# Input order, instruction order and the banks of the last output halves in a recurrence and feed-forward kernel on one core

## The chip, the core and the metric

The kernel runs on one core of a Trainium2 chip. A core has a matrix engine (PE, TensorE), a vector engine (DVE), a scalar engine (ACT), a general engine (POOL, GpSimd) and a queue engine (SP) that only issues transfers; each runs its own list of instructions in order, and semaphores hold an instruction until what it needs is done. Transfers between main memory and the on-chip SBUF are issued by SP and by POOL and carried by 16 DMA engines that all queues share. PE writes its results to PSUM, eight banks of 128 x 512 float32, from which DVE and ACT read. The metric is the device time of one execution in microseconds (us), lower is better.

## What is computed

A gated recurrence for 4 batches, 8 heads, 768 steps and head width 48, whose output goes, token by token, through a feed-forward layer of 384 to 2048 to 384 with SiLU:

```python
f = 1.0 / (1.0 + np.exp(-f_logit))
for t in range(S):
    state = f[:, :, t, :, None] * state + np.einsum('bhd,bhe->bhde', k[:, :, t], v[:, :, t])
    y[:, :, t] = np.einsum('bhd,bhde->bhe', q[:, :, t], state)
x = y.transpose(0, 2, 1, 3).reshape(B * S, H * D)
h = x @ w_in
out = (h * (1.0 / (1.0 + np.exp(-h)))) @ w_out
```

## The kernel before

The 768 steps of each batch are cut into six chunks of 128, so that there are 24 units (batch, chunk). Two units make a pair, and the 12 pairs are numbered 0 to 11. Pairs 0 to 3 hold two chunks of the same batch ("T" pairs, whose tokens are laid alternately over two slots); pairs 4 to 11 hold the same chunk of two batches. Within a chunk the recurrence is done with matmuls: the logarithm of the gate is summed along the chunk by a triangular matmul, q and k are scaled by the exponentials of that sum, scores of q against k are masked and applied to v, and a 48 x 48 state per head carries what came before.

The whole order of the kernel is written out by hand, in a table of words (`PLAN`, from line 37). A word is `kind.pair.part:engine:buffer`; the letters P, A, V, G and S stand for PE, ACT, DVE, POOL and SP. Each engine runs its own words in the order of the table. The kinds that matter here, with the line that issues them before the change:

- `f`, `k`, `q`, `v` (L241): a load of 384 KB from SP's queue, or half of one; `wi.n` and `wo.n` (L216, L219): a quarter of the first or second weight matrix, from POOL's queue, with a cast to bfloat16. Only the first four loads of the table are issued ahead of the setup of masks and constants.
- `E` (L248) and `L` (L260, L263): the exponential and the logarithm on ACT that make the log gate out of f. `cs` (L324 and L328 in T pairs, L331 and L334 in the others): its running sum on PE.
- `a`, `ia` (L336): the exponentials of that sum, on ACT; `al` (L278, L338): the decay over the whole chunk.
- `qg`, `ki` (L341): q times `a` and k times `ia`, on DVE or POOL. `vb`: v cast to bfloat16, on any of ACT, DVE and POOL.
- `tq` (L348): transposes of scaled q and k on PE; `qkc`: their copy out of PSUM on ACT or DVE (`qkD` has the DMA transpose them instead, L360).
- `sc` (L369, L373): scores; `at` (L377): their masking on DVE, in two halves per unit.
- `d` (L297, L406): a chunk's contribution to the state; `sd`, `su` (L410, L420): the state's update. `y`, `yi` (L285, L385, L389): the outputs of a chunk. `yc`, `yT`, `xc` (L397): cast, transpose and copy into the input of the feed-forward layer.
- `mi.P.j` (L271): the first weight matrix, 256 of the 2048 columns at a time; with a third number, for one unit of the pair only. `si` (L276): SiLU on ACT. `mo.P.i.n` (L306): a quarter of the second weight matrix. `oc`: the copy of the result out of PSUM; `so` (L316, L318): the store, from SP's or POOL's queue.
- `idle.512.n` (L465): n matmuls of zeros, 512 columns wide, whose result nobody reads.

For the last pair, `mo`, `oc` and `so` carry a further number: each of its two output tiles is made in two column halves of 192, and both halves of a tile lie in one bank of PSUM:

```python
nc.tensor.matmul(at("o", P, i)[:, cols], at("hT", P)[:, n, i * C:(i + 1) * C], w_out_sb[:, n, cols], start=(n == 0), stop=(n == NT - 1))
```

Of the kernel before, what the change touches and what calls it, by code (L numbers as in the profile page):

```python
# [41 lines left out]
tq.1.0:P:2 q.3.0:S:3 a.2.0:A:3 qg.1.1:G: sc.0.0:P:3,4 qkc.1.0:A:1 sc.0.1:P:6,7 at.0.0.1:V:0 k.3.0:S:3 wi.1:G: at.0.0.0:V: E.3.0:A:1 idle.512.2::5
tq.1.1:P:5 at.0.1.0:V:1 wi.2:G: d.1:P:1,4 qkc.1.1:A: v.2.0:S:2 su.1.0:V:0 wi.0:G: at.0.1.1:V: al.2:A:2 L.3.0:A:0 idle.512.3::2 sc.1.0:P:2,3 ki.2.0:G:4
sc.1.1:P:6,1 at.1.0.1:V:2 vb.0.0:A:2 cs.3.1:P:5 vb.0.1:A:3 at.1.1.0:V:3 qg.2.0:G: al.3:A:3 ia.2.1:A:2 d.0:P:7,3 at.1.1.1:V: a.2.1:A:0 cs.3.0:P:6
ia.3.1:A:4 su.0.0:V:0 qg.2.1:G:2 y.0:P:0,1 a.3.0:A:1 at.1.0.0:V: yc.0.0:A:0 yi.0.1:P: tq.2.0:P:7 a.3.1:A:3 wi.3:G: yc.0.1:V:1 ia.3.0:A:0 y.1:P:0,2
# [64 lines left out]
def kernel(  # L110
# [19 lines left out]
    NT = d_ff // 128  # L130
# [35 lines left out]
    for word in PLAN.split():  # L166
        name, eng, got = word.split(":")
# [257 lines left out]
    def takes(kind, rest):  # L425
# [22 lines left out]
        if kind == "mo":  # L448
            return [("o", *rest[:2])]
# [97 lines left out]
```

## Time and profile before

| what | before |
|---|---|
| median of 3 runs | 181.83 us |
| lowest and highest run | 181.17 and 182.06 us |
| the profiled execution's own time | 180.93 us |
| its span, first to last instruction | 179.2 us |
| PE busy in the span | 170.5 us (95%) |
| ACT, DVE, POOL busy | 132.7, 79.7, 61.6 us |
| granted TensorE clock | 1.000 |
| bytes moved | 31.91 MB |

PE is the busiest engine. A row of the profile that groups instructions gives the line, the engine, the operation, what is written and read, the count, the busy time and the mean time of one, and then the idle time of the engine just before these instructions. In rows by time, the first number is the start in us from the start of the span and the second the time until the group's end; consecutive instructions of one kind are merged. Instructions of one engine can overlap by about 0.1 us, so the distance from start to start is what one of them costs its engine.

### The profile page before, as it was taken

Reading aid. Unit: us, or ns where it says so; the run is one execution under the profiler, and the core shown is the slowest. Engines: PE = TensorE matmul, PEld = TensorE weight load, DVE = VectorE, ACT = ScalarE, POOL = GpSimd, SP = SyncE. Lnnn points to the kernel's source line nnn. Section 1 sums busy time; section 2 is a strip of 40 time slices with the busy share of each in tenths; the row PEclk is TensorE's granted clock in tenths of the full one; section 3 lists DMA queues with packets and bytes.
Section 4 is the critical chain, followed back from the end, with each engine's and each line's share of the span. In section 5 each row is a group of like instructions: output and inputs, shape, how many; then the busy total and the mean of one; then the engine's idle time right before and its main releaser. Section 6 shows DMA issues by size and latency. Waiting matters only on the chain.

```text
span 179.2 us, 4981 instructions
## 1 busy us (share of the span) xinstructions
PE 170.5 (95%) x2042; PEld 129.0 (72%) x2044; DVE 79.7 (44%) x166; ACT 132.7 (74%) x251; POOL 61.6 (34%) x106
## 2 busy tenths in 40 slices
PE   6769989999999999999999999999999999999993
PEld 2345779975788866778678877875876786788782
DVE  7078994008821246456673703342335747500002
ACT  3989983895289999999967558988796991178410
POOL 6036995000274004554044170636303592000010
PEclk9999999999999999999999999999999999999999
DMA  6999999999999799998478998994994496320043
GB/s 159 324 325 325 240 204 207 199 187 190 242 230 212 92 208 221 168 241 144 84 145 170 188 210 141 252 263 103 179 251 94 97 190 215 88 70 0 0 150 117
DMA packets 109366, 31.91 MB, mean 178 GB/s; under 512 B 103536, under 2 KB 108768, under 8 KB 109344
## 3 DMA queue, kind: packets, MB, share of 16 engines
q1 hardware_dynamic: 104464, 25.60, 70.2%
q0 software_dynamic: 4880, 6.00, 15.7%
q8 instruction: 16, 0.26, 0.6%
q14 instruction: 6, 0.05, 0.1%
HBM read 25.17 MB, written 4.72 MB: 167 GB/s over the span
## 4 chain that ended last, share of the span: by engine, by line
PE 77%; ACT 9%; DVE 4%; DMA 3%; SPq 2%; issue 1%; POOL 1%; DVEq 0%
PE pb L306 32%; PE pb L271 32%; ACT hT L276 4%; DMA q<-in_q_dram 3%; PE pb L373 2%; SPq L241 2%; PE pb L385 2%; PE pb L348 2%; PE pb L389 2%; DVE qk L341 2%; ACT L513 1%; DVE atm L377 1%; PE pb L331 1%; PE pb L397 1%; DVE st L420 1%
## 5 line engine op out<-in xcount | busy, mean ns | idle before, releaser
L306 PE MATMUL pb<-w_out_sb,hT 128*128 128x384 bf16 (+1 forms) x416 | 70.4, 314 | 0.2 <-ACT hT L276 0.2
L271 PE MATMUL pb<-xT,w_in_sb 128*128 128x256 bf16 (+1 forms) x672 | 68.9, 257 | 0.0
L271 PEld LDWEIGHTS <-w_in_sb 128*128 128x128 bf16 x672 | 56.6, 98 | 7.5 <-issue 0.3
L276 ACT ACTIVATE hT<-pb 128x512 bf16<-128x512 f32 x96 | 51.8, 617 | 12.4 <-PE pb L271 12.0
L306 PEld LDWEIGHTS <-hT 128*128 128x128 bf16 x416 | 37.7, 98 | 18.7 <-ACT hT L276 0.4
L377 DVE TENSOR_TENSOR atm<-pb,triu 128x512 bf16<-128x512 f32 x32 | 20.6, 684 | 20.5 <-PE pb L373 17.8
L336 ACT ACTIVATE x<-pb 128x384 f32<-128x384 f32 x48 | 22.1, 508 | 1.5 <-PE pb L331 1.4
L420 POOL TENSOR_TENSOR st<-sd,al 48x192 bf16<-48x192 f32 x32 | 16.6, 518 | 18.7 <-PE pb L385 12.1
L341 POOL TENSOR_TENSOR qk<-q,x 128x384 bf16<-128x384 f32 x11 | 11.3, 1025 | 31.9 <-ACT x L336 14.5
L513 ACT ACT_TABLE_LOAD x15 | 19.2, 1283 | 0.3
L185 ACT COPY ob<-pb 128x384 f32<-128x384 f32 (+1 forms) x15 | 6.8, 453 | 12.6 <-PE pb L306 12.6
L377 DVE TENSOR_TENSOR atm<-pb,mask 128x512 bf16<-128x512 f32 x16 | 10.2, 685 | 12.4 <-ACT hT L276 11.1
L187 DVE COPY ob<-pb 128x384 f32<-128x384 f32 (+1 forms) x11 | 5.8, 535 | 22.2 <-PE pb L306 22.2
L318 POOL DMA_DIRECT2D out_dram<-ob x8 | 4.6, 578 | 28.4 <-ACT ob L185 24.8
L316 POOL DMA_DIRECT2D out_dram<-ob x14 | 7.6, 548 | 19.6 <-DVE ob L187 15.9
L341 DVE TENSOR_TENSOR qk<-q,x 128x384 bf16<-128x384 f32 x13 | 7.6, 593 | 13.7 <-ACT x L336 13.7
L248 ACT ACTIVATE e<-f 128x768 f32<-128x768 f32 (+1 forms) x13 | 10.4, 800 | 4.4 <-DMA f<-in_f_logit_dram 4.2
L410 DVE TENSOR_TENSOR sd<-pb,st 128x384 f32<-128x384 f32 x16 | 8.9, 554 | 10.6 <-PE pb L406 3.9
L341 POOL TENSOR_TENSOR qk<-k,x 128x384 bf16<-128x384 f32 x10 | 10.8, 1082 | 6.4 <-ACT al L278 2.0
L185 ACT CAST yb<-pb 128x384 bf16<-128x384 f32 x12 | 5.6, 479 | 9.7 <-PE pb L389 9.6
L341 DVE TENSOR_TENSOR qk<-k,x 128x384 bf16<-128x384 f32 x14 | 9.9, 710 | 0.9 <-ACT x L336 0.9
L187 DVE CAST yb<-pb 128x384 bf16<-128x384 f32 x12 | 6.6, 556 | 8.0 <-PE pb L389 5.9
(72 smaller groups left out, 157.4 us busy)
## 6 DMA issues: line engine op xcount, KB each, us to landing
f<-in_f_logit_dram SPq DMA_DIRECT2D x11, 384.0 KB, 4.7
q<-in_q_dram SPq DMA_DIRECT2D x16, 192.0 KB, 4.1
v<-in_v_dram SPq DMA_DIRECT2D x16, 192.0 KB, 3.9
k<-in_k_dram SPq DMA_DIRECT2D x16, 192.0 KB, 3.9
k<-in_k_dram SPq DMA_DIRECT2D x4, 384.0 KB, 4.8
v<-in_v_dram SPq DMA_DIRECT2D x4, 384.0 KB, 9.5
q<-in_q_dram SPq DMA_DIRECT2D x4, 384.0 KB, 4.9
w_in_sb<-in_moe_w_in_dram POOLq DMA_DIRECT2D x4, 384.0 KB, 9.5
```

The costliest lines, as they stand in the source:

```text
L185: nc.scalar.copy(dst, src)
L187: ENG[eng].tensor_copy(dst, src)
L248: return nc.scalar.activation(e, at("f", P)[:, j * w:(j + 1) * w], AF.Exp, scale=-1.0)
L271: nc.tensor.matmul(h[:, i, cols], w_in_sb[:, kk, n * 128:(n + 1) * 128], at("xT", P)[:, kk, cols], start=(kk == 0), stop=(kk == KT - 1))
L276: return nc.scalar.activation(at("hT", P)[:, 2 * j:2 * j + 2, :], at("h", P, j).rearrange("p (n c) -> p n c", n=2), AF.Silu)
L306: nc.tensor.matmul(at("o", P, i)[:, cols], at("hT", P)[:, n, i * C:(i + 1) * C], w_out_sb[:, n, cols], start=(n == 0), stop=(n == NT - 1))
L336: nc.scalar.activation(at(kind, P, i).rearrange("p h d -> p (h d)"), at("cs", P, i)[:, 0:HD], AF.Exp, scale=1.0 if kind == "ia" else -1.0)
L341: ENG[eng].tensor_mul(at("qk", P, i)[:, j, :, 0:D], heads("qk"[j], P, i), at("ia" if j else "a", P, i))
L377: ENG[eng].tensor_mul(at("atm", P, i)[:, r], at(f"s{r}", P, i).rearrange("p (n c) -> p n c", c=C), mask[:, None, :].to_broadcast([C, NP, C]))
L410: nc.vector.tensor_add(at("sd", P, i), d_ps, prev_state(P, i))
L420: ENG[eng].tensor_mul(at("st", P, i)[lo:lo + D, :, r * D:(r + 1) * D], src[lo:lo + D, :, r * D:(r + 1) * D], al_of(P, i)[lo:lo + D, :, Non ...
L513: nc.scalar.preload_act_table_set(TABLES[mode])
```

## The change

The table is replaced by another one, and three lines of code give each half of the last pair's outputs a bank of its own. The counts of work stay as they are, but for these: 29 instead of 24 matmuls of zeros; of the copies out of PSUM, three `qkc` and four `xc` go from ACT to DVE and four `yc` from DVE to ACT; ten `vb` instead of five lie on POOL; two `ki` go from DVE to POOL; two stores go from POOL's queue to SP's; ACT has 13 loads of its function table behind the first one, where it had 15.

```diff
-f.2.0:S:0 k.0.0:S:0 f.0.1:S:1 f.0.0:S: E.2.0:A:0 f.1.0:S:2 L.2.0:A:0 v.1.0:S:0 q.0.0:S:0 idle.512.11::0 cs.2.1:P:0 E.0.1:A:1 E.0.0:A: k.1.0:S:1
...
-wo.0:G: ki.2.1:V: yc.1.0:A:2 yT.0.0:P:5 sd.0.1:V:0 yi.1.1:P: yT.0.1:P:1 yc.1.1:A:0 tq.2.1:P:6 xc.0.0:V:0 wo.1:G: xc.0.1:A: qkc.2.0:V:0 v.3.0:S:3
-yT.1.0:P:0 yT.1.1:P:3 xc.1.0:A:1 mi.0.2.0:P:2 qkc.2.1:V: su.0.1:G:0 xc.1.1:A: mi.0.3.0:P:5 mi.1.3.0:P:1 sd.1.1:V:1 mi.1.3.1:P: qg.3.0:V:3 wo.2:G:
...
+k.0.0:S:0 f.2.0:S:0 f.0.1:S:1 f.0.0:S: f.1.0:S:2 v.1.0:S:0 q.0.0:S:0 E.2.0:A:0 E.0.1:A:1 k.1.0:S:1 L.0.1:A:0 E.0.0:A: L.0.0:A: f.3.0:S:3
...
+yc.1.0:V:2 tq.2.0:P:4 yT.0.1:P:6 yi.1.1:P: wo.3:G: xc.0.1:V: yT.1.0:P:3 yc.1.1:A:0 sd.0.1:V:0 mi.0.2.1:P:6 al.3:A:3 ia.3.1:A:4 xc.1.0:V:1 mi.0.5.0:P:5
+wo.2:G: a.3.0:A:2 sd.1.1:V:1 mi.0.3.0:P:2 mi.1.4.0:P:3 qkc.2.0:V:0 qg.3.1:G:3 mi.0.5.1:P: v.5.1:S:4 mi.0.2.0:P: yT.1.1:P:7 su.0.1:G:0 mi.0.3.1:P:
+si.0.2:A:0 xc.1.1:V: mi.1.5.1:P:1 tq.2.1:P:0 su.1.1:G:0 mi.1.3.0:P:4 qkc.2.1:V: mi.1.3.1:P: mi.0.4.1:P:7 ki.3.0:G:0 mi.0.4.0:P: mi.1.5.0:P: si.0.4:A:
...
-                nc.tensor.matmul(at("o", P, i)[:, cols], at("hT", P)[:, n, i * C:(i + 1) * C], w_out_sb[:, n, cols], start=(n == 0), stop=(n == NT - 1))
+                nc.tensor.matmul(at("o", P, i, *rest[3:])[:, cols], at("hT", P)[:, n, i * C:(i + 1) * C], w_out_sb[:, n, cols], start=(n == 0), stop=(n == NT - 1))
...
-            copy(eng, at("ob", P, i)[:, cols], at("o", P, i)[:, cols])
+            copy(eng, at("ob", P, i)[:, cols], at("o", P, i, *rest[2:])[:, cols])
...
-            return [("o", *rest[:2])]
+            return [("o", *rest[:2], *rest[3:])]
```

In the new table the last `tq` of pair 2 (`tq.2.1`) and the last `yT` of pair 1 (`yT.1.1`) stand behind the first `mi` on PE, where they stood ahead of it.

The first place is SP's queue of loads, at its start. Buffers are named by kind and number: f_61, f_62, f_63 and f_64 take f of pairs 2, 0, 1 and 3, k_65 and q_71 are those of pair 0, k_66, q_72 and v_77 those of pair 1, v_78 that of pair 0. Before:

```order
L241 DMA f_61<-in_f_logit_dram 128x8x96
L241 DMA k_65<-in_k_dram 128x8x96
L241 DMA f_62<-in_f_logit_dram 128x4x96 x2
L241 DMA f_63<-in_f_logit_dram 128x8x96
L241 DMA v_77<-in_v_dram 128x8x96
L241 DMA q_71<-in_q_dram 128x8x96
L241 DMA k_66<-in_k_dram 128x8x96
L241 DMA q_72<-in_q_dram 128x8x96
L241 DMA f_64<-in_f_logit_dram 128x8x96
L241 DMA v_78<-in_v_dram 128x8x96
```

And with the change:

```order
L240 DMA k_65<-in_k_dram 128x8x96
L240 DMA f_61<-in_f_logit_dram 128x8x96
L240 DMA f_62<-in_f_logit_dram 128x4x96 x2
L240 DMA f_63<-in_f_logit_dram 128x8x96
L240 DMA v_77<-in_v_dram 128x8x96
L240 DMA q_71<-in_q_dram 128x8x96
L240 DMA k_66<-in_k_dram 128x8x96
L240 DMA f_64<-in_f_logit_dram 128x8x96
L240 DMA q_72<-in_q_dram 128x8x96
L240 DMA k_67<-in_k_dram 128x8x96
```

k of pair 0 and f of pair 2 change places at the head; f of pair 3 goes ahead of q of pair 1, and v of pair 0 goes from tenth place among whole loads to twelfth, behind k and q of pair 2.

The second place is ACT's list from its first exponential on. e_83 and lf_85 are the intermediate and the log gate of the pair loaded first; x is `a` or `ia`. Before:

```order
L248 ACTIVATE e_83<-f_61 128x768
L260 ACTIVATE lf_85<-e_83 128x8x2x48
L248 ACTIVATE e_84<-f_62 128x384 x2
L260 ACTIVATE lf_86<-e_84 128x4x2x48 x2
L248 ACTIVATE e_83<-f_63 128x768
L336 ACTIVATE x_88<-pb_142 128x384
L260 ACTIVATE lf_87<-e_83 128x8x2x48
L336 ACTIVATE x_89<-pb_143 128x384
L336 ACTIVATE x_90<-pb_143 128x384
L336 ACTIVATE x_91<-pb_144 128x384
L278 ACTIVATE al_128<-pb_145 128x8
L336 ACTIVATE x_92<-pb_142 128x384
```

And with the change:

```order
L247 ACTIVATE e_83<-f_61 128x768
L247 ACTIVATE e_84<-f_62 128x384
L259 ACTIVATE lf_85<-e_84 128x4x2x48
L247 ACTIVATE e_84<-f_62 128x384
L259 ACTIVATE lf_85<-e_84 128x4x2x48
L247 ACTIVATE e_84<-f_63 128x768
L259 ACTIVATE lf_86<-e_84 128x8x2x48
L335 ACTIVATE x_88<-pb_140 128x384
L335 ACTIVATE x_89<-pb_141 128x384
L335 ACTIVATE x_90<-pb_140 128x384
L335 ACTIVATE x_91<-pb_143 128x384
L259 ACTIVATE lf_87<-e_83 128x8x2x48
```

The exponential of pair 2's f still comes first; its logarithm (lf_87 now) goes from second place to twelfth, and the logarithm of pair 1 now comes ahead of the first `a`.

The third place is DVE's list from the masking of pair 0 to the last masking of pair 1; atm_111 and atm_112 belong to pair 0, atm_113 and atm_114 to pair 1, and st is the state. Before:

```order
L377 TENSOR_TENSOR atm_111<-pb_144,mask_159 128x512
L377 TENSOR_TENSOR atm_111<-pb_143,mask_159 128x512
L377 TENSOR_TENSOR atm_112<-pb_146,mask_160 128x512
L420 TENSOR_TENSOR st_149<-pb_141,al_128 48x4x48 x2
L377 TENSOR_TENSOR atm_112<-pb_147,mask_160 128x512
L377 TENSOR_TENSOR atm_113<-pb_143,mask_159 128x512
L377 TENSOR_TENSOR atm_114<-pb_146,mask_160 128x512
L377 TENSOR_TENSOR atm_114<-pb_141,mask_160 128x512
L420 TENSOR_TENSOR st_148<-pb_147,al_129 48x4x48 x2
L377 TENSOR_TENSOR atm_113<-pb_142,mask_159 128x512
```

And with the change:

```order
L419 TENSOR_TENSOR st_149<-pb_147,al_128 48x4x48 x2
L376 TENSOR_TENSOR atm_111<-pb_143,mask_160 128x512
L376 TENSOR_TENSOR atm_111<-pb_142,mask_160 128x512
L376 TENSOR_TENSOR atm_112<-pb_145,mask_159 128x512
L186 CAST vb_101<-v_78 128x384
L186 COPY qkTT_110<-pb_147 128x16x64
L376 TENSOR_TENSOR atm_112<-pb_146,mask_159 128x512
L419 TENSOR_TENSOR st_148<-pb_143,al_129 48x4x48 x2
L376 TENSOR_TENSOR atm_113<-pb_145,mask_160 128x512
L376 TENSOR_TENSOR atm_113<-pb_141,mask_160 128x512
L376 TENSOR_TENSOR atm_114<-pb_143,mask_159 128x512
L376 TENSOR_TENSOR atm_114<-pb_145,mask_159 128x512
```

The state of pair 1 (st_149) is updated first instead of after three maskings, and a cast of v and a copy of transposed q and k, which lay on ACT, stand between the maskings.

More of the change, by code (lines that the diff above doesn't have):

```diff
@@ L42 @@
[L42 to L45, printed above, removed]
@@ L106 @@
+mo.11.1.2.0:P: so.11.0.0:G: mo.11.1.2.1:P: mo.11.1.3.0:P: mo.10.0.3:P: oc.11.1.0:A:0 so.11.1.0:S: mo.11.0.0.1:P:7 oc.10.0:V:2 so.9.0:S: mo.11.1.3.1:P:
+so.10.0:S: mo.11.0.1.1:P: oc.11.1.1:V: mo.11.0.2.1:P: so.11.1.1:S: mo.11.0.3.1:P: oc.11.0.1:A: so.11.0.1:S:
 """
```

122 lines of the change are left out of this document (61 added, 61 removed).

## The prediction

> **What bounds the kernel now.** I read the page's first part, then the busy time by stretch, then the chain of waits, then the engines one by one through the first 25 us.
>
> ```profile
> PE 170.5 (95%) x2042; PEld 129.0 (72%) x2044; DVE 79.7 (44%) x166; ACT 132.7 (74%) x251; POOL 61.6 (34%) x106
> ```
>
> The busy time by stretch has, after the stretch and its length, the engines in this order: PE, weight loads, DVE, ACT, POOL.
>
> ```profile
> 10.00:15.00 5.00, 4.38 (x70) 2.65 (x72) 4.31 (x7) 4.51 (x13) 1.17 (x2) 1.00 1.17 325
> 15.00:20.00 5.00, 4.36 (x107) 2.93 (x97) 4.73 (x9) 5.00 (x11) 4.98 (x6) 1.00 1.18 306
> 20.00:25.00 5.00, 4.93 (x128) 4.50 (x127) 4.96 (x12) 4.85 (x12) 4.87 (x8) 1.00 1.21 205
> 40.00:60.00 20.00, 19.88 (x281) 15.28 (x272) 10.76 (x24) 13.86 (x27) 6.62 (x11) 1.00 1.03 212
> 60.00:80.00 20.00, 19.78 (x201) 13.61 (x198) 8.76 (x16) 19.88 (x39) 6.52 (x11) 1.00 1.11 188
> 170.00:175.00 5.00, 5.00 (x52) 4.22 (x50) 0.67 (x2) 0.64 (x2) 0.55 (x1) 1.00 0.45 157
> ```
>
> From 40 us on PE has hardly a gap: 0.12 + 0.22 us in the two stretches to 80 and nothing at the end; the stretches between show none either. Its work does not change, so there an order can give back about 0.34 us and no more, but a worse order can lose. The other place is the head, before the first matmul of the feed-forward layer, where PE runs zeros and waits. There DVE is the full engine (4.73 of 5, 4.96 of 5). The chain shows how it is fed:
>
> ```profile
> 5.24 4.81 DMA q<-in_q_dram
> 17.87 2.48 DVE atm L377 x4
> 21.82 0.52 PE pb L285 x32
> 22.79 0.17 PE pb L397 x3
> 22.95 0.45 PE pb L348 x8
> ```
>
> q of pair 0 lands at 10.05, DVE multiplies and masks, and PE can take the outputs of pair 1 (L285) once the last masking is done. On PE itself:
>
> ```profile
> 23.58 1.84 PE L271 MATMUL pb<-xT,w_in_sb 128*128 128x128 bf16 x30
> 26.72 0.36 PE L369 MATMUL pb<-qkTT 48*64 48x128 bf16 x11 [0.85 <-issue]
> ```
>
> The feed-forward layer starts at 23.58 and is stopped once more, for 0.85 us, inside one group of scores; "issue" says that the profile shows nothing that PE waited for.
>
> **The change part by part.** Most of it is the order of the head, so I rebuild that chain from starts in the trace. First ACT, which makes the factors DVE needs:
>
> ```profile
> 4.05 0.84 ACT L248 ACTIVATE e<-f 128x768 f32<-128x768 f32 x1 [2.03 <-DMA f<-in_f_logit_dram]
> 4.92 0.84 ACT L260 ACTIVATE lf<-e 128x768 bf16<-128x768 f32 x1
> 5.83 1.18 ACT L248 ACTIVATE e<-f 128x384 f32<-128x384 f32 x2
> 6.91 0.92 ACT L260 ACTIVATE lf<-e 128x384 bf16<-128x384 f32 x2
> 7.73 0.83 ACT L248 ACTIVATE e<-f 128x768 f32<-128x768 f32 x1
> 8.47 0.47 ACT L336 ACTIVATE x<-pb 128x384 f32<-128x384 f32 x1
> 8.84 0.83 ACT L260 ACTIVATE lf<-e 128x768 bf16<-128x768 f32 x1
> 9.57 1.24 ACT L336 ACTIVATE x<-pb 128x384 f32<-128x384 f32 x3
> 12.02 0.91 ACT L336 ACTIVATE x<-pb 128x384 f32<-128x384 f32 x2
> ```
>
> *The two first loads swapped.* A load is 393 KB and the queue moves 325 GB/s (first row of the stretches), 1.21 us each. ACT's first exponential waited for f of pair 2 until 4.05; as second load that f lands at 5.26, and ACT's list still begins with it, so all behind it starts late. From 5.26: a full exponential costs ACT 0.74 until the next independent operation (7.73 to 8.47); a logarithm that needs the exponential just ahead comes 0.55 (half width) or 0.87 (4.05 to 4.92) after it; other half-width ones follow at about 0.42; a logarithm costs 0.73 (8.84 to 9.57); an `a` or `ia` 0.37 (8.47 to 8.84). Then: halves of pair 0 at 6.00, 6.55, 6.98, 7.53; pair 1 at 7.95 and 8.82; the first `a` at 9.55 (8.47 before). Three more `a` and `ia` to 10.66, the moved logarithm of pair 2 at 11.03, three `ia` from 11.76, half a us (estimated from the `ia` steps, since both are no longer than one) for `al` and a cast of v, and `a` of pair 1 at 13.35, ending at 13.84. Before, it was the second of the pair at 12.02 and ended at 12.93. So the factor of pair 1 comes 0.9 us later.
>
> *DVE from there.*
>
> ```profile
> 10.62 0.55 DVE L341 TENSOR_TENSOR qk<-k,x 128x384 bf16<-128x384 f32 x1
> 11.09 0.55 DVE L341 TENSOR_TENSOR qk<-q,x 128x384 bf16<-128x384 f32 x1
> 11.56 1.36 DVE L341 TENSOR_TENSOR qk<-k,x 128x384 bf16<-128x384 f32 x1
> 12.84 0.68 DVE L187 COPY qkTT<-pb 128x1024 bf16<-128x1024 bf16 x1
> 13.44 0.54 DVE L341 TENSOR_TENSOR qk<-q,x 128x384 bf16<-128x384 f32 x1
> 17.12 0.72 DVE L420 TENSOR_TENSOR st<-pb,al 48x192 bf16<-48x192 f32 x2 [0.17 <-PE pb L297]
> 17.87 2.48 DVE L377 TENSOR_TENSOR atm<-pb,mask 128x512 bf16<-128x512 f32 x4
> 20.27 0.71 DVE L420 TENSOR_TENSOR st<-pb,al 48x192 bf16<-48x192 f32 x2
> 21.02 0.69 DVE L377 TENSOR_TENSOR atm<-pb,mask 128x512 bf16<-128x512 f32 x1
> 21.63 0.55 DVE L187 CAST yb<-pb 128x384 bf16<-128x384 f32 x1
> ```
>
> q times `a` of pair 1 starts at 13.87, k times `ia` 0.47 later (10.62 to 11.09), ending at 14.89. `d` of pair 1 follows on PE, and the state's update, which is now ahead of the maskings on DVE, starts 0.62 after it:
>
> ```profile
> 16.50 0.52 PE L297 MATMUL pb<-vb,qk 64*128 64x96 bf16 x16
> ```
>
> (16.50 to 17.12), that is at 15.53. From here DVE has no hole that I can find: two updates at 0.75 (17.12 to 17.87), eight maskings at 0.60 (17.87 to 20.27, four), and the two pieces that came over from ACT, a cast at 0.46 (priced as the cast at 21.63, to the next start at 22.09) and a copy of 1024 columns at 0.60 (12.84 to 13.44). Sum 1.50 + 4.80 + 0.46 + 0.60 = 7.36, so the last masking ends at 22.98 instead of 21.71: 1.27 later. Behind it come `y` of pair 1 (0.63 until its end, 21.71 to 22.34 in the chain's L285 row), the cast (0.55), a transpose and the first `mi` (0.25 with hand-overs): 24.45, say **24.5 instead of 23.58, +0.92**. It makes up 0.35 of the 1.27 because `mi` no longer waits for the transposes that were moved behind it.
>
> *Work moved behind the start.* `tq.2.1` and `yT.1.1` now come after the first `mi`: 0.45 and 0.17 (chain rows at 22.95 and 22.79). PE is full from there, so **+0.62**.
>
> *The stop of 0.85.* The scores of pair 2 where it fell now come some 9 us later, among matmuls of 128 columns. It can vanish (-0.85) or come back elsewhere (0). I take **-0.5**, nearer to vanishing, since dense groups of small matmuls no longer follow one another there.
>
> *ACT's relief.* Two table loads (1.28 each, by the chain) and some copies leave ACT, which is full from 60 to 80. PE loses only 0.22 us in that stretch. Between 0 and -0.34 over all; I take **-0.1**.
>
> *The rest at nothing.* The five more matmuls of zeros lie in waits: five at 0.40
>
> ```profile
> 1.37 4.37 PE L465 MATMUL pb<-zero,triu 128*128 128x512 bf16 x11 [1.37 <-POOL triu masks.py:66]
> ```
>
> (4.37 for 11) end by 7.8, and the first `cs` cannot start before the second half logarithm ends, at 8.05; without that cover, up to 2 us. The halves in banks of their own end no wait, since PE is 5.00 of 5.00 busy in the last stretch and the store after the last matmul is the same.
>
> Sum: 0.92 + 0.62 - 0.5 - 0.1 = +0.94, about **+1.0 us**. The profiled execution took 180.93 (span 179.2), 0.9 below the median of 181.83; I carry the difference to the median: **182.8**.
>
> *A rule beside it.* The row at 11.56 took 1.36 where its neighbours take 0.55, and POOL's multiplication ran from 11.44 to 12.50:
>
> ```profile
> 11.44 1.06 POOL L341 TENSOR_TENSOR qk<-k,x 128x384 bf16<-128x384 f32 x1 [2.04 <-ACT al L278]
> 15.83 2.46 POOL L216 DMA_DIRECT2D w_in_sb<-in_moe_w_in_dram  x3
> ```
>
> The Trainium skill, page "SBUF — State Buffer", section "Who interferes with whom", says that a DVE instruction with two SBUF inputs and a GpSimd instruction that reads SBUF exclude each other for a whole instruction; the row agrees. By that rule the larger share of POOL speaks against the change: if POOL's cast of v follows its multiplication without letting DVE in, k times `ia` of pair 0 slips, and the sum would be 0.4 us higher. Without it the sum stands as above.
>
> **The rivals.** *The weights collide with the inputs* (slower, and more). POOL's three requests for the first weight go out right after k times `ia` and a cast, and no longer behind a second multiplication: `ia` of pair 1 ends at 12.3, the multiplication takes 1.06, the cast about half of that, so at 13.9 instead of 15.83. When weights flow, SP's loads crawl:
>
> ```profile
> k<-in_k_dram SPq DMA_DIRECT2D x4, 384.0 KB, 4.8
> v<-in_v_dram SPq DMA_DIRECT2D x4, 384.0 KB, 9.5
> DMA to landing us min/median/max: 3.3/4.9/22.9
> ```
>
> In whole loads v, which holds the two issued last, needs 9.5 us in the median against k's 4.8, and the worst load of the first 40 us 22.9. Started 1.9 us earlier, the weights catch q and k of pair 3 as well, and v of pair 0, now two places later. PE reaches the first transposes of pair 3 behind 28 half-width `mi` (0.34 each, five of them in the L271 row) and 0.9 us of other groups, at 34.9. If k of pair 3 falls into the crawl and lands after about 32.8, POOL's two multiplications (2.1 us) delay them one for one. I price it at 2 us: **184.8**. Against it: the weights also end 1.9 us earlier. The Trainium skill, page "DMA: Bandwidth & Descriptors", under "Arbitration", has each DMA engine alternate between queues packet by packet, which would give this crawl from the first weight packet on; the v row agrees.
>
> *No loss in the head, and PE's gaps closed* (faster). If f of pair 2 is not late, because the first two loads run side by side, DVE needs no hole: its work from its first multiplication at 10.8 on (six at 0.47, the copies 1.20, the cast 0.46, the rest 6.30) ends at 21.6, `mi` starts at 23.1 to 23.25, and with the moved work that is +0.2. Then the stop (-0.85) and the gaps (-0.34) give -1.0: **180.8**. It decides from the point where the first `a` starts by 8.6. Against it: q of pair 0 waited its full turn in the queue (4.81 us).
>
> *It evens out* (no change). The head loses 0.9 to 1.2 in all, the stop vanishes whole: **182.0**. That the banks and the order do nothing visible ends here too.
>
> **How the numbers follow.** Forecast 0.45 (own range 182.3 to 183.6: the stop kept or gone, the lock taken or not), collision 0.15, evens out 0.23, faster 0.17. I call no change what lies within 0.5%, 0.9 us, about what a measurement of this kernel can tell: 180.9 to 182.7. Of the forecast's 0.45 a part of 0.10 falls in it. Faster 0.17; same 0.23 + 0.10 = 0.33; slower 0.35 + 0.15 = 0.50. The range goes from the faster case to the collision: 180.7 to 184.8.
>
> **What would show it.** Right: ACT's first exponential at about 5.25, the first `a` at 9.5, the state's update at 15.5, the last masking of pair 1 ending near 23.0, the first L271 at 24.5, and no PE gap over 0.3 us after it. Wrong: a first exponential near 4.1, DVE through by 22, or PE idle over half a us between 30 and 50 with its releaser on POOL or a load. If the time falls while L271 starts late, PE's gaps were larger than its busy rows say, and my bound of 0.34 us is at fault.

## The result and the profile after

| | before | with the change |
|---|---|---|
| median, in alternating runs on one chip | 181.76 us (4 runs) | 188.56 us (4 runs) |
| the profiled execution's own time | 180.93 us | 188.4 us |
| its span | 179.2 us | 186.6 us |
| first feed-forward matmul starts | 23.58 us | 29.22 us |
| from there to the end of the span | 155.6 us | 157.4 us |
| granted TensorE clock, mean | 1.000 | 0.981 |

The ratio is 1.038 (95% interval 1.035 to 1.041): slower, as forecast, but by 6.8 us instead of 1.0, and far above the range of 180.7 to 184.8. Of the span's 7.4 us, 5.6 are lost before the first feed-forward matmul and 1.8 behind it. One execution each of the runs a2, b2, e1 and i1 below was slow as a whole, at a lower granted clock; the ratios leave these out, the medians do not, and a2's profile is of such an execution (204.36 us, clock 0.855), so that its start, in brackets in the table, is not compared.

The page's first line of busy time shows that PE is busy 175.3 us instead of 170.5, with five matmuls of zeros as its only additional work, and that it waits more as well (94% of the span, it was 95):

```profile
PE 175.3 (94%) x2048; PEld 130.9 (70%) x2049; DVE 82.3 (44%) x165; ACT 127.2 (68%) x243; POOL 65.2 (35%) x111
```

The stretches from 15 us on, with the columns as in the prediction (PE, weight loads, DVE, ACT, POOL, then the granted clock, the share of the DMA engines and GB/s):

```profile
15.00:20.00 5.00, 3.21 (x75) 2.14 (x74) 4.95 (x8) 2.75 (x6) 4.96 (x8) 1.00 1.20 280
20.00:25.00 5.00, 3.47 (x85) 2.36 (x85) 4.83 (x8) 2.05 (x5) 3.12 (x4) 0.76 1.19 205
25.00:30.00 5.00, 5.00 (x81) 4.36 (x80) 2.81 (x8) 2.15 (x7) 4.32 (x6) 0.56 1.21 205
```

Before, PE was busy 4.36 of 5.00 in the first of these stretches, and the clock stayed at 1.00 throughout. Now it is busy 3.21, and in the two stretches behind, the clock is granted at 0.76 and 0.56. In stretches of 1 us the clock reads 0.50 in every one from 23 to 29 us, so that PE ran at half speed for some 2.4 us of the one stretch and 4.4 of the other. In the last, PE is busy all the time, but at half speed, so part of what reads as full there is loss.

By time, ACT has the first `a`, and `a` of pair 1:

```profile
9.86 1.66 ACT L335 ACTIVATE x<-pb 128x384 f32<-128x384 f32 x4
13.72 0.54 ACT L335 ACTIVATE x<-pb 128x384 f32<-128x384 f32 x1
```

DVE from the multiplication of k of pair 1 to the last masking:

```profile
14.82 1.35 DVE L340 TENSOR_TENSOR qk<-k,x 128x384 bf16<-128x384 f32 x1
16.10 0.68 DVE L186 COPY qkTT<-pb 128x1024 bf16<-128x1024 bf16 x1
16.70 0.71 DVE L419 TENSOR_TENSOR st<-pb,al 48x192 bf16<-48x192 f32 x2
17.44 1.89 DVE L376 TENSOR_TENSOR atm<-pb,mask 128x512 bf16<-128x512 f32 x3
19.24 1.90 DVE L186 CAST vb<-v 128x384 bf16<-128x384 f32 x1
23.00 2.71 DVE L376 TENSOR_TENSOR atm<-pb,mask 128x512 bf16<-128x512 f32 x4
```

POOL beside it:

```profile
13.66 0.83 POOL L186 CAST vb<-v 128x384 bf16<-128x384 f32 x1
14.44 2.47 POOL L215 DMA_DIRECT2D w_in_sb<-in_moe_w_in_dram  x3
...
19.11 0.78 POOL L218 DMA_DIRECT2D w_out_sb<-in_moe_w_out_dram  x1
19.91 1.00 POOL L340 TENSOR_TENSOR qk<-k,x 128x384 bf16<-128x384 f32 x1
```

And PE, which waits for that cast inside `d` of pair 0 (L296), then makes `y` of pair 1 and starts the feed-forward layer:

```profile
18.85 0.34 PE L296 MATMUL pb<-vb,qk 64*128 64x96 bf16 x8
21.19 0.35 PE L296 MATMUL pb<-vb,qk 64*128 64x96 bf16 x8 [2.00 <-DVE vb L186]
...
26.60 0.82 PE L284 MATMUL pb<-vb,atm 64*128 64x48 bf16 x32
...
29.22 2.25 PE L270 MATMUL pb<-xT,w_in_sb 128*128 128x128 bf16 x36
```

DVE's other eight casts of v in this profile take 0.35 in six places, and 0.67 and 1.15 in two; this one took 1.90. It started 0.13 after a weight request and ended 0.23 after POOL's next multiplication (19.91 to 20.91). PE had nothing to do until the cast was through, and from about 22.6 on its clock was lower.

Late in the kernel there is one new stop. On PE, scores of pair 11 wait for ACT; on ACT, the copy that must free their bank waits for a store; and the chain of waits names that store:

```profile
157.86 0.38 PE L372 MATMUL pb<-qkT 48*128 48x128 bf16 x7 [0.93 <-ACT ob L184]
```

```profile
157.33 0.48 ACT L184 COPY ob<-pb 128x384 f32<-128x384 f32 x1 [1.44 <-DMA out_dram<-ob]
```

```profile
152.35 4.90 DMA out_dram<-ob
```

The store takes 4.9 us to land, while POOL issues six more transfers of this kind between 151.97 and 155.25; the copy needs its buffer.

### The profile page after: what moved, and what is told of

Same layout as the page of the kernel before. It is cut to its first block, busy times and chain, and to the rows that moved or that the text cites. A ratio compares the mean times of both kernels' runs of the same rounds, so it can differ in the third digit from the quotient of the medians.

```text
span 186.6 us, 5001 instructions
## 1 busy us (share of the span) xinstructions
PE 175.3 (94%) x2048; PEld 130.9 (70%) x2049; DVE 82.3 (44%) x165; ACT 127.2 (68%) x243; POOL 65.2 (35%) x111
## 4 chain that ended last, share of the span: by engine, by line
PE 79%; ACT 8%; DMA 5%; DVE 5%; issue 1%; SPq 0%; DVEq 0%; ACTq 0%
PE pb L270 33%; PE pb L305 32%; DMA out_dram<-ob 3%; ACT x L335 2%; DMA f<-in_f_logit_dram 2%; PE pb L372 2%; PE pb L384 2%; DVE atm L376 2%; PE pb L347 2%; PE pb L388 1%; ACT lf L259 1%; PE pb L396 1%; ACT e L247 1%; PE pb L330 1%; PE pb L405 1%
## 5 line engine op out<-in xcount | busy, mean ns | idle before, releaser
L184 ACT CAST yb<-pb 128x384 bf16<-128x384 f32 x16 | 7.8, 486 | 17.0 <-PE pb L388 11.3
L340 POOL TENSOR_TENSOR qk<-k,x 128x384 bf16<-128x384 f32 x12 | 12.1, 1016 | 11.8 <-ACT x L335 8.8
L186 POOL CAST vb<-v 128x384 bf16<-128x384 f32 x10 | 5.7, 583 | 23.9 <-DMA v<-in_v_dram 23.7
L340 DVE TENSOR_TENSOR qk<-k,x 128x384 bf16<-128x384 f32 x12 | 8.7, 722 | 8.4 <-ACT x L335 8.4
L317 POOL DMA_DIRECT2D out_dram<-ob x6 | 3.4, 567 | 25.1 <-ACT ob L184 25.1
L464 PE MATMUL pb<-zero,triu 128*128 128x512 bf16 x28 | 8.9, 466 | 1.4 <-POOL triu masks.py:66 1.4
L340 DVE TENSOR_TENSOR qk<-q,x 128x384 bf16<-128x384 f32 x13 | 8.7, 679 | 2.0 <-ACT x L335 1.2
```

What stands on the lines that cost most here:

```text
L184: nc.scalar.copy(dst, src)
L186: ENG[eng].tensor_copy(dst, src)
L340: ENG[eng].tensor_mul(at("qk", P, i)[:, j, :, 0:D], heads("qk"[j], P, i), at("ia" if j else "a", P, i))
L464: nc.tensor.matmul(buf["pb", int(got)][:, 0:rest[0]], triu, zero[:, 0:rest[0]], start=True, stop=True, skip_group_check=True)
```

## The experiments

All runs in one table; "ratio" is against runs of the kernel before on the same chip (their medians lie between 181.25 and 181.53), with the 95% interval. "First mi" is the start of the first feed-forward matmul in the profiled execution.

| run | built on | median us | ratio | first mi us |
|---|---|---|---|---|
| a1_cast_on_act | change | 186.83 | 1.029 (1.024 to 1.033) | 27.69 |
| a2_zeros_ahead_of_d | change | 186.73 | 1.028 (1.024 to 1.032) | (27.67) |
| a3_f_first | change | 186.90 | 1.030 (1.027 to 1.034) | 28.27 |
| a4_other_output_buffer | change | 188.16 | 1.037 (1.033 to 1.040) | 29.22 |
| d2_store_earlier | change | 187.21 | 1.032 (1.028 to 1.036) | 29.05 |
| d1_cast_on_act_and_warm | change | 185.31 | 1.021 (1.018 to 1.024) | 25.95 |
| f1_three_causes | d1 and d2 | 184.38 | 1.013 (1.011 to 1.016) | 26.42 |
| f2_and_log_first | f1 | 184.03 | 1.013 (1.009 to 1.017) | 25.90 |
| g1_pool_order | f2 | 184.27 | 1.016 (1.012 to 1.020) | 25.88 |
| g2_banks_and_transpose | g1 | 183.50 | 1.013 (1.009 to 1.017) | 25.88 |
| i1_fewer_zeros | g2 | 183.77 | 1.013 (1.011 to 1.016) | 24.95 |
| b1_k_first | before | 181.74 | 1.001 (0.999 to 1.003) | 23.94 |
| b2_cast_on_dve | before | 182.14 | 1.004 (1.002 to 1.006) | 24.31 |
| b3_two_banks | before | 181.34 | 0.999 (0.997 to 1.001) | 24.56 |
| e1_q_ahead_of_k | before | 181.36 | 1.000 (0.998 to 1.002) | 23.43 |
| h1_scores_later | before | 181.50 | 1.001 (0.999 to 1.004) | 23.72 |
| i2_first_request | before | 182.21 | 1.005 (1.003 to 1.006) | 24.63 |
| g3_weights_early | before | 186.17 | 1.026 (1.023 to 1.030) | 29.24 |

### The cast, the clock and the first load

a1 moves the cast of v of pair 0 from DVE back to ACT; a2 leaves it and puts nine matmuls of zeros into PE's wait; a3 loads f of pair 2 first again.

```diff
-vb.0.1:V:3
+vb.0.1:A:3
```

```diff
-qkc.1.1:V: d.0:P:3,2
+qkc.1.1:V: idle.512.9::1 d.0:P:3,2
```

```diff
-k.0.0:S:0 f.2.0:S:0 f.0.1:S:1
+f.2.0:S:0 k.0.0:S:0 f.0.1:S:1
```

> The change, with the cast of the second half of v of pair 0 on ACT again instead of DVE. Theory 1 (this cast waited on DVE for POOL, 1.90 us instead of 0.5, held up the state contribution of pair 0 on PE for 2.2 us, and the wait let the TensorE clock fall): the first L270 starts near 26 instead of 29.2, the clock stays at 1.00 from 20 to 30, and the time falls by about 3 us to 185.5. Theory 2 (the head is late because the two first loads were swapped): at most 0.5 us less, 188.

> The change, with nine more matmuls of zeros on PE just ahead of the state contribution of pair 0, where PE otherwise waits 2.2 us for the cast on DVE; nothing on DVE, ACT or POOL moves. If the fallen clock has a price of its own: clock 1.00 from 20 to 30, first L270 near 27.4, time 186.7 (1.8 us less). If only the wait counts and the clock is a bystander: the clock stays up, the first L270 stays near 29, the time at 188.5.

> The change, with f of pair 2 loaded ahead of k of pair 0 again. Theory 2 (the load swap set the head back): ACT's first exponential at 4.05 instead of 5.43, everything up to the masking 1.2 us earlier, time at 186 or less. Theory 1 (the cast on DVE behind POOL): ACT starts 1.2 us earlier, but the cast still waits for POOL and the first L270 comes forward by no more than 0.5 to 1 us: 187.6 to 188.

a1 gives back 1.7 us (by the ratios, 0.0096 of 181.5), with the cast at 0.51 on ACT. In its profile the clock still falls, to 0.80 and 0.86, behind a stretch in which PE is busy 3.84:

```profile
15.00:20.00 5.00, 3.84 (x87) 2.61 (x87) 4.95 (x9) 3.10 (x7) 4.96 (x8) 1.00 1.20 280
20.00:25.00 5.00, 3.59 (x82) 2.43 (x81) 3.67 (x7) 2.05 (x5) 4.83 (x6) 0.80 1.20 207
25.00:30.00 5.00, 4.82 (x104) 4.44 (x103) 3.06 (x7) 3.81 (x8) 3.80 (x7) 0.86 1.22 205
```

The clock does not fall every time: over the whole execution it was 1.000 in two of a1's four runs (186.23 and 186.50 us) and 0.99 in the other two (187.16 and 187.62).

a2 gives back 1.8 us with the cast where it was, and the clock was 1.000 in the three runs other than the profiled one: keeping the clock up is worth that. So the cast and the clock are two losses. In the change the clock fell in all four runs, behind the stop that the cast makes.

a3 was to tell what the late f costs. Its first `a` comes at 9.74, only 0.12 earlier than in the change: ACT, done with the first exponential, waits for f of pair 0 instead. But its time fell by 1.5 us, and the reason is another. Three rows, from DVE and from POOL:

```profile
19.13 0.35 DVE L186 CAST vb<-v 128x384 bf16<-128x384 f32 x1
```

```profile
19.01 0.78 POOL L218 DMA_DIRECT2D w_out_sb<-in_moe_w_out_dram  x1
19.81 1.01 POOL L340 TENSOR_TENSOR qk<-k,x 128x384 bf16<-128x384 f32 x1
```

The same cast, starting 0.12 after the same request where it was 0.13 in the change, went through at once. What lets it through is not shown. The starts do not tell it: in a4 and d2, whose order in the head is that of the change, the same cast started 0.12 and 0.11 after the request and took 1.91 and 1.92 (first row a4, second d2).

```profile
19.22 1.91 DVE L186 CAST vb<-v 128x384 bf16<-128x384 f32 x1
19.10 1.92 DVE L186 CAST vb<-v 128x384 bf16<-128x384 f32 x1
```

The Trainium skill, page "SBUF — State Buffer", section "Who interferes with whom", says that a cast can enter a mode in which it needs the port that DVE shares with GpSimd, and that whoever issues first holds it for the whole instruction. A wait until POOL's instruction is over agrees with it (the cast of the change ended 0.23 after one); that it lasted through two of them, the request and the multiplication, is more than the page says.

### The late store

a4 gives the waiting copy another output buffer (0 for 2, and 2 to the next user of 0); d2 issues one store (`so.7.0`) earlier on POOL and gives the copy the buffer that it frees.

```diff
-oc.6.1:A:2
-oc.8.0:V:0
+oc.6.1:A:0
+oc.8.0:V:2
```

```diff
-qkD.10.0:S:0 su.9.0:G:0
+qkD.10.0:S:0 so.7.0:G: su.9.0:G:0
...
-so.7.0:G: si.9.7:A: yD.10.1:S:3 y.10.0:P:3 oc.6.1:A:2
+si.9.7:A: yD.10.1:S:3 y.10.0:P:3 oc.6.1:A:1
```

> The change, with the output copy of the second unit of pair 6 in the buffer of the first unit of pair 6 and the one of the first unit of pair 8 in the other's place: the copy at 157.3 no longer waits for the store issued at 152.35. If that wait is what stops PE for 0.93 us inside the scores at 156.7: the gap is gone and the time is 0.9 us less, 187.6. If the store of the other buffer is as late: no change, 188.5.

> The change, with the store of the first unit of pair 7 issued on POOL some 6 us earlier, as soon as POOL's list allows, and its buffer taken by the output copy of the second unit of pair 6. If that copy waits for a store wherever one was issued late, and PE's 0.93 us at 156.7 with it: the gap goes, 187.6. If the gap is PE's own: it stays, 188.5.

a4 failed: the other buffer's store is in the same crowd, and the copy starts as late.

```profile
157.47 0.48 ACT L184 COPY ob<-pb 128x384 f32<-128x384 f32 x1 [1.28 <-DMA out_dram<-ob]
```

In d2 the copy starts at 155.46 without a wait, PE's stop is gone, and the ratio falls from 1.038 to 1.032: 1.1 us. The two intervals touch, but the four runs (186.95 to 187.47) all lie below those of the change (188.40 to 188.98).

```profile
155.46 0.48 ACT L184 COPY ob<-pb 128x384 f32<-128x384 f32 x1
```

### Together

d1 has the cast on ACT, as in a1, and enough zeros to keep PE busy; f1 adds the earlier store, as in d2. The zeros are these:

```diff
-idle.512.3::7 d.1:P:7,0
+idle.512.7::7 d.1:P:7,0
...
-sc.1.0:P:3,5
+idle.512.5::3 sc.1.0:P:3,5
```

> The change, with that cast on ACT and with nine more matmuls of zeros in PE's two other waits of the head (four ahead of the state contribution of pair 1, five ahead of the second scores of pair 1). If cast and clock are the two causes and add up: first L270 near 25.5, clock 1.00 throughout, 185.0 (3.5 us less than the change). If the cast's gain was only the clock's, or the other way round: 186.7, as with either alone.

> The change with the cast of v on ACT, the zeros that keep PE warm and the earlier store, all three. If the costs are separate and add up (185.3 with the first two, the store 0.9 to 1.3): 184.0 to 184.4, no gap over 0.5 us at 150 to 160. Rival: the store's wait only moves to another store, 185.0 to 185.4, with a gap over 0.5 us after 140 that has an output store behind it.

d1's stretches (the clock is the third number from the end):

```profile
15.00:20.00 5.00, 4.56 (x90) 2.88 (x89) 4.96 (x9) 3.12 (x7) 4.96 (x8) 1.00 1.20 279
20.00:25.00 5.00, 4.93 (x135) 3.50 (x135) 4.31 (x9) 3.08 (x8) 4.84 (x6) 1.00 1.20 207
25.00:30.00 5.00, 4.25 (x75) 3.95 (x73) 2.81 (x7) 3.43 (x7) 4.70 (x8) 1.00 1.22 206
```

The clock holds, and 3.2 us are back, where a1 and a2 alone gave 1.7 and 1.8. With the store it is 4.5 of 6.9 (by the ratios, of 181.5). That these three cost time is shown by undoing them; how much of the 3.2 belongs to the cast and how much to the clock is known only roughly. d1 (185.31) is also 1.1 us faster than a1's two runs at full clock, so the zeros give back something besides the clock there: a1's profile has a stop of 0.88 in the scores of pair 1 (its row is shown further below) that d1's has not. 2.4 us stay.

### The rest of the head

Four runs took more suspects away, each run built on the one before it. f2 loads f of pair 2 first and puts its logarithm behind its exponential, as before. g1 restores POOL's order (the cast of v of pair 1 first, the weight requests behind its second multiplication, whose factor ACT makes later). g2 exchanges two banks (1 and 5, from there to the end of the table) so that scores of pair 1 wait for an earlier masking, and moves the last `yT` two `mi` forward. i1 takes away zeros that had become too many, and has POOL cast v of pair 0 ahead of the third weight request.

```diff
-E.2.0:A:0 E.0.1:A:1
+E.2.0:A:0 L.2.0:A:2 E.0.1:A:1
```

```diff
-ki.1.0:G:2 ... vb.1.1:G:1 ... wi.1:G: ... wi.2:G: ... wi.0:G: ... qg.1.1:G:
+vb.1.1:G:1 ki.1.0:G:2 ... qg.1.1:G: wi.1:G: wi.2:G: wi.0:G:
```

```diff
-sc.1.0:P:3,5 ... cs.3.0:P:1 ... mi.1.4.0:P:3 ... mi.0.5.1:P: ... mi.0.2.0:P: yT.1.1:P:7
+sc.1.0:P:3,1 ... cs.3.0:P:5 ... mi.1.4.0:P:3 yT.1.1:P:7 ... mi.0.5.1:P: ... mi.0.2.0:P:
```

```diff
-idle.512.7::7 d.1:P:7,0
+idle.512.3::7 d.1:P:7,0
...
-idle.512.5::3 sc.1.0:P:3,1
+idle.512.2::3 sc.1.0:P:3,1
...
-wi.1:G: wi.2:G: wi.0:G: ... vb.0.0:G:2
+wi.1:G: wi.2:G: vb.0.0:G:2 wi.0:G:
```

> The same with f of pair 2 loaded first again and its logarithm right behind its exponential on ACT, as before. If the late factor of pair 1 is the rest of the loss in the head (prediction's term 0.9): the factor `a` of pair 1 starts 0.7 to 1.2 us earlier than in the run with three causes, first feed-forward matmul near 25.0, 183.0 to 183.3. Rival: the blocked multiplication of k of pair 1 beside the weight requests and the bank that the scores wait for set the start, whatever ACT does: first matmul near 25.9, 184.0 to 184.4.

> The run with f and its logarithm first (184.0), with POOL's list in the head as before: the cast of v of pair 1 ahead of its first multiplication, the first three weight requests behind q of pair 1, whose factor ACT makes later. If DVE's long rows (1.36, 0.85, 1.36 beside POOL's multiplication, cast and requests) are the rest of the loss in the head: two of the three rows go to 0.55, the state's update starts 0.9 to 1.2 us earlier than 16.50, first feed-forward matmul at 24.8 to 25.1, 182.9 to 183.3. Rival: the scores of pair 1, which wait for a bank, and the stop of 0.76 at 28.4 eat it: first matmul within 0.3 of 25.90, 183.7 to 184.2.

> The same, with banks 1 and 5 exchanged from the last scores of pair 1 on, so that these wait for the masking before the last and not for the last, and the last transpose of y of pair 1 three feed-forward groups earlier. If these two are the last pieces of the loss (0.48 in DVE's list, 0.76 on PE): 1.0 to 1.3 below the run without them, so 181.7 to 182.1 if that one comes at 183.0, and no PE gap over 0.3 us between 26 and 31. Rival: the weights or PE's own list set the place, and a gap over 0.5 us opens elsewhere before 32: less than 0.6 below.

> The run with exchanged banks (183.5), with three matmuls of zeros ahead of the first `d` instead of seven, two ahead of the last scores of pair 1 instead of five, and the cast of v of pair 0 on POOL ahead of the third weight request. If the zeros that kept PE warm now hold up the state's update (16.33, where its multiplication is ready at 14.95) and the scores: the update starts at 15.6 to 15.8, the first feed-forward matmul at 25.1 to 25.4, clock 1.000, 182.6 to 183.0. Rival: PE falls cold again without them, 20 to 30 us at a clock below 0.8, 184.0 to 185.5. Rival two: the landing of v of pair 0 (about 17.6) holds `d` of pair 0 and all behind it, first matmul within 0.2 of 25.88, 183.3 to 183.7.

None of the four moves the ratio beyond its interval (1.013, 1.016, 1.013, 1.013, where f1 has 1.013); the profiles show why. f2's ACT is earlier, but DVE then meets POOL in three places instead of one, and the first `mi` moves by 0.5. In g1 two of these rows are 0.55 again, as expected, and the start does not move at all: now the state's update waits for PE, which is busy with the zeros put there to keep it warm.

```profile
14.42 0.55 DVE L340 TENSOR_TENSOR qk<-k,x 128x384 bf16<-128x384 f32 x1
14.88 0.68 DVE L186 COPY qkTT<-pb 128x1024 bf16<-128x1024 bf16 x1
16.33 0.72 DVE L419 TENSOR_TENSOR st<-pb,al 48x192 bf16<-48x192 f32 x2 [0.76 <-PE pb L296]
```

g2 removes the 0.59 that PE waited until 29.41 for the late transpose; its median is 0.8 us lower and its ratio 0.003 (0.5 us), with intervals that overlap. The banks give nothing: the scores start at 22.28 in both runs, behind zeros that stand ahead of them. i1 then starts the update at 15.53 and the layer at 24.95 with the clock at 1.00, as its first theory said, and its time does not fall. After six matmuls PE waits for the second piece of the weights:

```profile
24.95 0.49 PE L270 MATMUL pb<-xT,w_in_sb 128*128 128x128 bf16 x6 [0.18 <-DVE xT L186]
26.17 1.18 PE L270 MATMUL pb<-xT,w_in_sb 128*128 128x128 bf16 x18 [0.72 <-DMA w_in_sb<-in_moe_w_in_dram]
```

The change's order of `mi` needs that piece in its second group; before, it came in the sixth. The requests that go out late enough not to meet DVE's multiplications bring it too late for this order. Of i1's 2.5 us of span over before, 1.4 are the later start, 0.7 this wait and 0.6 the moved work (as predicted), less the old stop of 0.85, which makes 1.9. The other 0.6 lie in PE's busy time behind the start (152.63 us for 151.41, of which 0.6 are the moved work) and are not assigned. Of the later start, PE still waits 0.72 at 18.47 for POOL's cast of v of pair 0; no run puts this cast, or the load of that v, back in its old place.

### Single edits to the kernel before

b1 swaps the first two loads, b2 puts the cast of v of pair 0 on DVE, b3 gives the last halves two banks, e1 loads q of pair 1 ahead of k, h1 moves three `mi` ahead of the scores in which PE stopped, and g3 and i2 move two and one of the weight requests ahead of POOL's second multiplication (i2 also has DVE's multiplication of k of pair 1 ahead of its copy).

```diff
# b1
-f.2.0:S:0 k.0.0:S:0 f.0.1:S:1
+k.0.0:S:0 f.2.0:S:0 f.0.1:S:1
# b2
-vb.0.1:A:3
+vb.0.1:V:3
# h1
-mi.0.2.1:P: sc.2.1:P:7,0
+mi.0.2.1:P: mi.1.5.1:P:4 mi.0.3.1:P: mi.1.5.0:P: sc.2.1:P:7,0
# g3
-qg.1.1:G: ... wi.1:G: ... wi.2:G:
+wi.1:G: wi.2:G: qg.1.1:G:
```

> The kernel before with k of pair 0 loaded ahead of f of pair 2, nothing else. My prediction's term: every exponential of the head starts 0.9 to 1.2 us later (first one at 5.26 instead of 4.05), the first `a` at about 9.5, the first feed-forward matmul near 24.5, 182.4 us beside 181.5. Rival, from the run with f first (the swap was worth 0.1 us there, because the next half exponential waits for f of pair 0, landing at 5.8 in either order): the first `a` within 0.3 us of the 8.47 of before, the start within 0.3 of 23.58, 181.5 to 181.8. The tuned place: the long row of k times ia beside POOL may shift either way by 0.8.

> The kernel before, with one part of the change: the cast of the second half of v of pair 0 on DVE, between two maskings, instead of on ACT. POOL multiplies at that time (18.3 to 21.3). Theory 1 (a cast on DVE waits for POOL): the cast takes over 1 us, the last masking of pair 1 ends at 23 instead of 21.7, the clock may fall, time 183 or more. If a DVE cast beside POOL costs its 0.5 us only: 182, the time of before plus 0.5.

> The kernel before with the halves of the last output in banks 3 and 4. My prediction's term: nothing, 181.5 (within 0.3), since PE is busy 5.00 of 5.00 in the last stretch; the two last groups of matmuls and the two copies keep their durations. Rival: the last copy overlaps the last matmuls better and the end comes 0.2 to 0.4 earlier, 181.1 to 181.3.

> The kernel before, with q of pair 1 loaded ahead of k of pair 1. The row of 1.36 us on DVE at 11.56 ran while POOL multiplied k of pair 1, which it could do as soon as that k had landed. With k one place later, POOL starts at 12.6, when DVE is through: the DVE row takes 0.55, the scores of pair 0 start near 14.1 instead of 14.6, and the time falls by up to 0.5 us (0.3 if the first weight, landed at 23.2, becomes the bound). If the long row had another cause: no change, or slower by the wait of POOL for k.

> The kernel before with three groups of six feed-forward matmuls moved ahead of the two scores of pair 2 in which PE stops for 0.85. If the stop belongs to the scores or to their time (my prediction: dense small matmuls): it stays five matmuls into the second scores, or goes, and with it 0.85 us: 180.7 to 181.0. If it belongs to a place in PE's list counted in instructions: it falls 18 matmuls nearer to the scores' start, three into the first scores, with about the same length, and the time is 181.4 to 181.8.

> The kernel before with two requests for the first weight moved ahead of POOL's multiplication of q of pair 1, so that they go out beside DVE's multiplications, as in the change. If a request holds the lock as a multiplication does: one of the DVE rows at 13.44 and 13.91 takes 1.3 instead of 0.55, and the first feed-forward matmul comes 0.4 to 0.9 later than 23.58; 181.9 to 182.5. If requests do not block (what DVE waited for in the change was the cast of v, or another POOL row): both rows at 0.55, 181.3 to 181.8.

> The kernel before with only the first weight request ahead of POOL's multiplication of q of pair 1, and k times ia of pair 1 on DVE ahead of its copy, so that it starts inside this request. If the first request holds it, as the row of 1.35 in the change suggests: a row of 1.2 to 1.4 at about 12.85, and the first feed-forward matmul 0.3 to 0.8 later than 23.58, 181.6 to 182.3. If a request does not hold a multiplication: 0.55 there, start within 0.3 of 23.58, 181.2 to 181.6, and what blocked that row in the change stays open.

b1: the first `a` comes at 9.36, 0.89 late, close to the chain that I predicted (9.55, 1.08 late); the first `mi` is 0.36 late and the time 0.2 (0.1%, within the interval). ACT had 0.48 of idle time ahead of a copy at 13.41, and it took up the rest. b2: the cast takes 0.49 and is not blocked, though POOL multiplies from 18.65 to 21.69 beside it, and the time is 0.4% up: the cast on DVE costs its own length there, not 1.9.

```profile
19.40 0.49 DVE L187 CAST vb<-v 128x384 bf16<-128x384 f32 x1
```

b3: no change. e1: DVE's row of 1.36 falls to 0.55, as expected, but the next multiplication now meets POOL's, which starts at 12.68, and takes 1.06 for 0.54. The masking starts at 15.17 (15.06 before): the wait went to the next row, so e1 does not tell what it is worth.

```profile
13.03 1.06 DVE L341 TENSOR_TENSOR qk<-q,x 128x384 bf16<-128x384 f32 x1
```

h1 did not decide. The moved `mi` met the second weight piece that had not landed (0.56 of idle time at 26.11, where the weight loads of these matmuls are the ones that wait for the requests), and after this wait no stop was left to place.

g3 is the surprise. DVE's two multiplications were not blocked (0.54 and 0.55 beside the second request), so on that the second theory is right; but the kernel lost 4.9 us, which neither foresaw. POOL waits 6.50 for q of pair 2 (last row):

```profile
12.64 1.71 POOL L216 DMA_DIRECT2D w_in_sb<-in_moe_w_in_dram  x2
15.10 0.99 POOL L341 TENSOR_TENSOR qk<-q,x 128x384 bf16<-128x384 f32 x1 [0.74 <-ACT x L336]
16.04 0.79 POOL L216 DMA_DIRECT2D w_in_sb<-in_moe_w_in_dram  x1
16.86 1.01 POOL L341 TENSOR_TENSOR qk<-k,x 128x384 bf16<-128x384 f32 x1
24.36 1.95 POOL L341 TENSOR_TENSOR qk<-q,x 128x384 bf16<-128x384 f32 x2 [6.50 <-DMA q<-in_q_dram]
```

Weights that leave 3.2 us earlier (12.64 instead of 15.83) catch the input that is next in SP's queue, and PE stands for 3.8 us; behind that its clock is 0.66 from 25 to 30 us, so the 4.9 are the wait and the clock together. In the change the requests left at 14.44 and q of pair 2 was not caught; that it loads this q one place earlier, ahead of v of pair 0 instead of behind it, may be the reason, and was not tried.

i2: the multiplication of k of pair 1 started 0.39 after the first request, as far inside it as in the change, and took 0.55 (13.34 to 13.88 by the trace). A single request did not hold it. i2 is still 0.8 us slower than before (by the ratio), which neither theory foresaw: with one request at 12.95, POOL already waits 2.06 for q of pair 2 at 20.99, and the old stop in the scores of pair 2 lasts 1.43. How much each of the two costs was not separated.

## Why the prediction was wrong

- **"From here DVE has no hole that I can find."** This step failed. I priced twelve pieces by their lengths (7.36 us), the cast at 0.46, and the last masking to end 7.45 after the update's start (15.53 to 22.98). It ended 9.01 after it (16.70 to 25.71): the cast took its engine 1.82 from start to start, 1.36 more than priced, and the last four maskings 0.23 more, where the scores ahead of them wait for a bank and run at half clock. The price came from a wrong row: the cast at 21.63 reads PSUM, while the one that moved reads v in SBUF. The rows of that kind in the trace of before give the warning. Eleven casts of v on DVE have a median of 0.35 and a longest of 1.15, and one that starts 0.13 after a request of POOL (116.39 to 116.96) takes 0.69 and ends 0.25 after the request. (The first row gives the shortest, the median and the longest in ns.)

```profile
L187 DVE CAST vb<-v x11: 350/352/1148, 42.0 to 144.0; 128x384 bf16<-128x384 f32 x11
116.52 0.69 DVE L187 CAST vb<-v 128x384 bf16<-128x384 f32 x1
116.39 0.57 POOL L318 DMA_DIRECT2D out_dram<-ob  x1 [1.37 <-ACT ob L185]
```

  I had named the lock in "a rule beside it", but asked only whether it would move one multiplication; a1 shows what the moved cast cost, 1.7 us.
- **The clock had no term.** I took 1.47 us from the last masking to the first `mi`, from rows at full clock; it took 3.51, at a clock of 0.50. a2, with zeros in the stop, gave back 1.8 us. My chain said that DVE would be the full engine to 23 us with PE waiting for it, and PE's thinner stretch (3.21 for 4.36) follows from that; I did not ask what a thinner PE does.
- **The late factor** (term 0.92). In the change ACT's factor was 1.3 late (`a` of pair 1 ends at 14.26 for 12.93 before and 13.84 predicted), and the update came another 0.8 late through the row of 1.35. But b1, with the same swap alone, lost 0.2 us, within its interval, and f2, which undid it, won 0.1 to 0.4: the chain on ACT was right, and how much of it idle time elsewhere covers was not counted. So the term that stood for the loss in the head is the smallest part of it.
- **The moved work** (0.62) and **the banks** (nothing) hold: in the change the moved groups take 0.17 and 0.44 on PE from start to start (31.31 and 32.51), and b3 shows the banks.
- **The stop of 0.85** went from its place, where I took -0.5 for it; but a stop of the same kind stands earlier, inside the scores of pair 1, in a1 and, shorter, in f1:

```profile
23.14 0.31 PE L368 MATMUL pb<-qkTT 48*64 48x128 bf16 x2 [0.88 <-issue]
```

```profile
22.89 0.36 PE L368 MATMUL pb<-qkTT 48*64 48x128 bf16 x11 [0.19 <-issue]
```

  In a1 two matmuls of the group are left when it comes (in a3 too), in f1 eleven, and f1 has nine more zeros ahead of it. In before, b1, b2, b3, e1 and i2 it comes with eleven matmuls of the scores of pair 2 left, for 0.75 to 1.43 us. That speaks for a place counted in PE's list, and not for the dense groups of small matmuls that I argued with; but d1, with the same list as f1 in the head, shows no stop, and h1, which was to decide it on the kernel before, did not. Its cause stays open.
- **"A worse order can lose"** stood in the text without a price. It was 1.1 us (d2), by a store that lands too late, which I had no term for since the trace of before has no such wait.
- **The collision of weights and inputs** did not come in the change, whose requests left 1.4 us earlier than before (14.44 for 15.83; I had 13.9). As a mechanism it is real and can be dearer than my 2 us: 4.9 in g3, the fallen clock included, with requests 3.2 us earlier and q of pair 2 as the input hit.

What stays open: what held DVE's multiplication for 1.35 us in the change (14.82). It began inside the first of three requests in a row, and so did a row of 1.36 in f2 (13.98); beside one request (i2) or the second of two (g3) a multiplication was not held. Open too: why the cast passed in a3, and 0.6 us of i1.

No version ran faster than before. In i1 the last limit that was met is the change's order of `mi` against the landing of the weights.

## What to carry to other kernels

When an instruction moves to another engine, price it from rows of that engine with the same operands, and look at the longest of them and at what the neighbour did beside it, not only at the usual one: here 0.46 became 1.9 beside a weight request (and stayed 0.49 in b2, where POOL was multiplying). Price what waits for it as well: the thinner PE behind it paid as much again in its clock. When an order is changed to start work earlier, look at what lands next, weights, inputs and stores alike: 0.7 us in i1, 0.9 in the change and 4.9 in g3 were transfers that nobody had waited for before. And when a cause is found, undo it alone and then with the others, since each wait removed here laid bare the next, the zeros against the clock among them.

## What the hardware showed that I had not expected

- The clock fell with PE busy 3.21 of 5 us and with no stop longer than the 2.00 at 21.19. In the stretch from 15 to 20 us, every profile but a2's with 3.84 or less lost the clock behind it, and every one with 4.08 or more kept it. But this is no general threshold: before has 3.24 from 5 to 10 us, and i2 3.57 from 25 to 30, with a clock of 1.00 in the stretch behind, while b3, whose head is that of before, has 3.56 from 5 to 10 and 0.66 behind it in its profile. Together with a1's four runs this says that the same list of instructions can keep or lose the clock from one execution to the next. The Trainium skill, page "TensorE: Matmul & The Clock Gate", section "Why this matters for your kernels", asks for no idle gap of PE over some 3 us; the stops here were shorter, so the trace goes beyond this rule (g3, with a stop of 3.77 us and 0.66 behind it, agrees with it).
- Of five profiles in which the same cast on DVE started 0.11 to 0.13 us after the same request of POOL, four have it at 1.90 to 1.92 us and one at 0.35, and the starts do not tell them apart.
- A store from SP's queue took 4.9 us to land with six more issued by POOL beside it; the nine of its queue and size take 2.0 us in the median.
